# Batch 1's sums of q and k by pairs of tokens, raw weights by pairs of units, and fixed orders in the front of a fused attention and feed-forward kernel

## The chip, the core and the metric

The kernel runs on one core of a Trainium2 chip. Its time is the device time of one execution in microseconds (us). The core's engines are named as in the profile: PE (matrix products; PEld is its loading of weights), DVE (vector), ACT (activation functions), POOL (GpSimd) and SP (which here only starts transfers). Each works through its own queue in order, and they wait for one another by semaphores. All arithmetic is in float32; a product of full precision is made of three products of `fp32r` parts.

## What is computed

```
q_d, k_d, v_d = means of q, k, v over 4 neighbouring tokens       # q: (4 batches, 8 heads, 576 tokens, 64)
out_up    = repeat(softmax(q_d k_d^T / 8) v_d, 4)
out_local = softmax(q k^T / 8 where |i - j| < 4) v
x = (out_up + out_local) as (2304, 512)
x = (silu(x Wgate) * (x Wval)) Wout                               # inner width 1536
h = x Win;  out = (h * clip(h + 3, 0, 6) / 6) Wout2               # inner width 2048
```

The inputs are float64 in the reference; the five weight matrices reach the chip as 8-byte numbers, of which the kernel keeps the upper bits.

## The kernel before

**Blocks and units.** The 2304 tokens are cut into five blocks (512, 384, 512, 512 and 384 tokens). A block runs through 68 units, each a 128-wide piece of a weight matrix: G (gate), V (value), O (out), H, P, two of a kind after each other (G0 G1 V0 V1 G2 G3 V2 V3 O0 O1 ...). A unit of G, V or H over 512 columns is 12 products `pG`, `pV`, `pH` on PE.

**A unit's weights.** In block 0 a unit passes five steps that `prefetch(i)` gives out: `load_raw` (SP, into one of four `w64` buffers, in the page `w`), `decode_a` (ACT, `top`), `decode_b` (DVE, which joins the bits into `w32` and gives the `w64` buffer back), a write to HBM for the later blocks (`kept`, from ACT's queue), and, by pairs of units, `split_unit` (`wr`: the high part on ACT, the rest on DVE).

**The front.** `first_batch` makes batch 0's attention on PE before the units begin. `load_T` turns q and k; `down_scores`, `down_trans` and `down_values` (`fdS`, `fdT`, `fdO`) are the attention of the means, two heads at a time (c = 0 to 3). The local attention goes over five tiles of 122 tokens (the last has 88): `scores(i)` (`fS` on PE, its maximum `fnm` on DVE, eight exponentials into `held` on ACT), `norm(i)` (DVE), `trans(i)` (some filler products and the transposes `fPT` on PE, copied to `turned` by ACT and DVE), `values(i)` (`fO` on PE, then `xr` by ACT and DVE: the columns of the first block). The filler products compute nothing that is used; `FILL_P` says how many stand ahead of each `trans(i)`. PSUM has eight banks: `acc0` to `acc3`, two `mm`, `pa` and `px`. `down_trans` and `down_values` both use `pa` and `px`, `values` one of them; `fS` takes `acc0` and `acc1` or the two `mm`; `fPT` takes `acc2` and `acc3`, and each G or V unit one `mm`.

**Order.** A scheduler orders each engine's instructions when the program is built. Those that go through `tc.keep_in_program_order` (in `late`, `behind`, `together`) keep the order in which the code gives them; `behind` does so while `front[0]` is true.

**Batch 1's sums of 4** (`down_sums`) come from POOL's queue: the first of four tokens is loaded into `dn`, the other three are added to it by accumulating loads. Their transposes `pqT` and `pkT` follow on PE among the first units.

Of the kernel before, what the change touches and what calls it, by code (L numbers as in the profile page):

```python
# [32 lines left out]
HALVES = 1  # L33
# [10 lines left out]
FILL_P = (4, 8, 8, 8, 8)  # L44
# [3 lines left out]
def tile_kernel(  # L48
# [86 lines left out]

    def behind(ins):

        if front[0]:
            tc.keep_in_program_order(ins)
# [26 lines left out]
    def view(t, i):  # L166
        return t[:, i % 2, :].rearrange("p (c e) -> p c e", c=NC)

# [8 lines left out]
    def load_unit(i):  # L177
# [12 lines left out]
        if kind in "GVH":  # L190
            src = src[:, f * P * m:(f + 1) * P * m].rearrange("(c p) f -> p c f", p=P)
        else:
            src = src[f * P:(f + 1) * P, :].rearrange("p (c e) -> p c e", c=NC)
        if wide:
            raw[i] = sp.tile([P, 4 * DM + 32], I16, tag="w64", name=f"w64_{i}", bufs=4)
            behind(nc.sync.dma_start(raw[i][:, 1:1 + 4 * DM].rearrange("p (c e) -> p c e", c=NC), src))
        else:
            nc.sync.dma_start(view(w32[i // 2], i), src)
# [34 lines left out]
    def split_unit(i):  # L233
        if i % 2:
            return
        s = w32[i // 2].rearrange("p u (c e) -> p u c e", c=NC)
        r = sp.tile([P, 2, 2, NC, P], F32R, tag="wr", name=f"wr{i}", bufs=3)
        behind(nc.scalar.activation(r[:, :, 0], s, AF.Copy))  # L238
        behind(nc.vector.tensor_tensor(r[:, :, 1], s, r[:, :, 0].bitcast(F32), op=ALU.subtract))  # L239
        split[i], split[i + 1] = r[:, 0], r[:, 1]  # L240
# [29 lines left out]
    def put_cols(bi, col, xv):  # L270
# [4 lines left out]
        nc.scalar.activation(dst[:, :, 0], xv, AF.Copy)  # L275
        nc.vector.tensor_tensor(dst[:, :, 1], xv, dst[:, :, 0].bitcast(F32), op=ALU.subtract)
# [39 lines left out]


    def first_batch():
# [6 lines left out]
        with tc.tile_pool(name="fp", bufs=1) as fp:  # L325
# [125 lines left out]
            for base, sgn in ((-UPAD, -1), (UPAD + 3, 1)):  # L451
# [3 lines left out]
                )  # L455
            kT = fp.tile([P, NC, S + 6], F32, name="fkT")
            nc.vector.memset(kT[:, :, :3], 0.0)
            nc.vector.memset(kT[:, :, S + 3:], 0.0)
# [12 lines left out]
            def load_T(w, c):  # L471
                src = qn[w, c // 2]
                for th in range(2):
# [13 lines left out]
                    if w == "q":  # L487
                        nc.vector.tensor_scalar(dst, ps[:, :, :TT], 0.125, None, op0=ALU.mult)
                        nc.scalar.activation(small, ps[:, :, TT:], AF.Copy, scale=1 / 128)
                    else:  # L490
                        nc.scalar.activation(dst, ps[:, :, :TT], AF.Copy)
                        nc.vector.tensor_copy(small, ps[:, :, TT:])
# [7 lines left out]
            def down_scores(c):  # L500
# [14 lines left out]
                for par in range(2):  # L515
                    nc.vector.tensor_reduce(nm[:, par], pss[par], axis=AX.X, op=ALU.max, negate=True)
                    for half in range(2):
                        nc.scalar.activation(
# [6 lines left out]
            def down_trans(c):  # L525
                pd = dst[c]
                for par in range(2):
# [3 lines left out]
                    nc.scalar.activation(dpt[h], pt, AF.Copy)  # L531

            def down_values(c):
# [9 lines left out]
                nc.vector.tensor_scalar(sd, po[:, :, :, D:], EPS, 4.0, op0=ALU.add, op1=ALU.mult)  # L543
                nc.vector.reciprocal(sd, sd)
                nc.vector.tensor_tensor(
                    odN[:, :, 2 * c * D:2 * (c + 1) * D].rearrange("p g (a d) -> p g a d", a=2),
                    po[:, :, :, :D], sd.to_broadcast([NJH, 2, 2, D]), op=ALU.mult,
                )

# [4 lines left out]
            first_max = []  # L554

            def scores(i):
# [27 lines left out]
                for par in range(2):  # L584
                    ps = pss[par][:n, :, :w_]
                    nc.vector.tensor_reduce(nm[:n, :, par], ps, axis=AX.X, op=ALU.max, negate=True)
                    for c in range(NC):
                        nc.scalar.activation(
                            p_[:n, c, par, :w_], ps[:, c], AF.Exp, bias=nm[:n, c, par:par + 1],
                            accum_out=sm[:n, c, par:par + 1],  # L590
                        )
                pe[i], tot[i] = p_, sm
                if i == 0:
                    first_max.append(nm[:n, 0, :1])

            def norm(i):
                n = size(i)
                w_ = n + 6
                nc.vector.tensor_scalar(tot[i][:n], tot[i][:n], EPS, None, op0=ALU.add)
                nc.vector.reciprocal(tot[i][:n], tot[i][:n])  # L600
                nc.vector.tensor_tensor(
# [8 lines left out]
            def trans(i):  # L610
# [3 lines left out]
                for hh in range(2):  # L614
# [9 lines left out]
                    if hh:  # L624
                        nc.vector.tensor_copy(to, ps[:w_, :, :, :n])
                    else:
                        nc.scalar.activation(to, ps[:w_, :, :, :n], AF.Copy)
# [27 lines left out]
            for c in range(NC):  # L655
# [6 lines left out]
                if c == 2:  # L662
                    prefetch(3 - LR)
# [12 lines left out]
            down_trans(3)  # L676
            down_values(2)
            norm(1)
            scores(2)
            down_values(3)  # L680
            prefetch(5 - LR)
            values(0)
            for i in range(1, NT):
                next(ahead, None)
                next(ahead, None)
                trans(i)
                if i + 2 < NT:
# [5 lines left out]
                if i + 1 < NT:  # L693
                    norm(i + 1)
                next(ahead, None)
                values(i)
            for _ in ahead:
                pass
        front[0] = False
# [240 lines left out]
    HIGH, LOW = ((0, 0), (1, 0)), ((0, 1),)  # L940

    def run_unit(i):
# [3 lines left out]
        if kind in "GVH":  # L946
            ps = bank("mm", f"p{kind}{bi}_{f}", 2)[:, :nt]
            x = xr[bi] if kind != "H" else state["x2"]
            cols = [slice(0, nt)]
            if i < HALVES:  # L950
                cols = [slice(0, 244), slice(244, nt)]
            for cs in cols:
                for part in (HIGH, LOW):
# [203 lines left out]
```

## Time and profile before

| | |
|---|---|
| median of 3 runs | 967.41 us (967.27 to 970.9) |
| the profiled execution | 967.38 us |
| its span, first to last instruction | 965.7 us |
| PE busy, mean granted clock | 948.1 us, 0.993 |
| DVE, ACT, POOL busy | 724.6, 501.6, 110.4 us |

The time is the device's, the span runs from the first to the last instruction of the core; 1.7 us lie around it. A timeline row gives start, length (with the tail of the last instruction), engine, line, operation, result and inputs, shapes and count, and in brackets how long the engine had stood idle and what ended that. The granted clock is a share of 2.4 GHz.

### The profile page before, as it was taken

How to read it: one execution, taken by the hardware profiler on the slowest of the kernel's cores; microseconds unless marked ns; L12 is line 12 of the kernel's file. 1: busy time of each engine (PE TensorE's matmuls, PEld its weight loads, DVE VectorE, ACT ScalarE, POOL GpSimd, SP SyncE). 2: the span in 40 equal slices, each digit the busy share in tenths (PEclk: the TensorE clock that was granted, in tenths of full speed). 3: DMA queues.
4: the chain of work that ended last, by engine and by line, in shares of the span. 5: the costliest groups of instructions: out<-in, count | busy, mean ns of one | idle time of the engine just before them, and what ended most of it. 6: DMA issues, size and time to landing. Idle time of an engine off the chain costs nothing.

```text
span 965.7 us, 13166 instructions
## 1 busy us (share of the span) xinstructions
PE 948.1 (98%) x4928; PEld 803.2 (83%) x4928; DVE 724.6 (75%) x1059; ACT 501.6 (52%) x928; POOL 110.4 (11%) x125
## 2 busy tenths in 40 slices
PE   9899999999999999999999999999999999999997
PEld 7687888777899988878888778888888788999996
DVE  4678976899979979999774799997337994445652
ACT  4666566876543567553333764443335445444542
POOL 7610002200062300014320000000000000000000
PEclk9999999999999999999999999999999999999999
DMA  8999799866799823359972222462322323443331
GB/s 195 228 270 340 247 366 311 183 198 236 261 246 264 166 86 109 99 188 242 199 157 88 88 67 67 173 216 90 97 100 93 103 88 108 154 131 130 120 122 33
DMA packets 116340, 160.80 MB, mean 167 GB/s; under 512 B 61868, under 2 KB 83756, under 8 KB 116276
## 3 DMA queue, kind: packets, MB, share of 16 engines
q1 hardware_dynamic: 67892, 131.41, 42.7%
q0 software_dynamic: 43488, 10.72, 11.1%
q10 hardware_dynamic: 4896, 17.83, 4.7%
q8 instruction: 39, 0.64, 0.3%
q14 instruction: 25, 0.20, 0.1%
HBM read 137.29 MB, written 22.54 MB: 166 GB/s over the span
## 4 chain that ended last, share of the span: by engine, by line
PE 78%; DVE 7%; DMA 1%; ACT 1%; issue 1%; ACTq 0%; DVEq 0%
PE pH L956 19%; PE aP L998 18%; PE aO L998 13%; PE pV L956 13%; PE pG L956 12%; DVE wr L239 2%; PE pS L881 1%; PE pO L731 1%; DMA w<-in_moe_w_out_dram 1%; DVE xf L856 1%; PE pPT L724 1%; PE px L847 1%; DMA w<-in_moe_w_gate_dram 1%; DVE pv L827 1%; DVE w L225 1%
## 5 line engine op out<-in xcount | busy, mean ns | idle before, releaser
L239 DVE TENSOR_TENSOR wr<-w,wr 128x1024 fp32r<-128x1024 f32 x170 | 207.8, 1222 | 123.8 <-ACT wr L238 123.6
L238 ACT ACTIVATE wr<-w 128x1024 fp32r<-128x1024 f32 x170 | 179.5, 1056 | 119.1 <-issue 57.7
L956 PE MATMUL pH<-x,wr 128*128 128x512 f32 (+1 forms) x960 | 212.2, 372 | 0.0
L998 PE MATMUL aP<-wr,gH 128*128 128x512 f32 x864 | 211.4, 395 | 0.3 <-ACT gH L973 0.3
L956 PEld LDWEIGHTS pH<-x,wr 128*128 128x128 f32 x960 | 173.1, 188 | 25.3 <-issue 2.9
L998 PEld LDWEIGHTS aP<-wr,gH 128*128 128x128 f32 x864 | 159.8, 188 | 34.8 <-issue 2.5
L956 PE MATMUL pG<-xr,wr 128*128 128x512 f32 (+3 forms) x732 | 156.4, 369 | 1.0 <-DVE sl L968 0.6
L956 PE MATMUL pV<-xr,wr 128*128 128x512 f32 (+1 forms) x720 | 153.9, 369 | 0.9 <-ACT sl L962 0.9
L998 PE MATMUL aO<-gV,wr 128*128 128x512 f32 (+1 forms) x720 | 154.4, 371 | 0.0
L956 PEld LDWEIGHTS pG<-xr,wr 128*128 128x128 f32 x732 | 133.3, 191 | 18.5 <-DVE sl L968 1.0
L998 PEld LDWEIGHTS aO<-gV,wr 128*128 128x128 f32 x720 | 132.4, 190 | 16.9 <-DVE gV L974 0.2
L956 PEld LDWEIGHTS pV<-xr,wr 128*128 128x128 f32 x720 | 130.8, 188 | 18.4 <-ACT sl L962 1.8
L971 ACT ACTIVATE h<-pH,consts 128x512 f32<-128x512 f32 (+1 forms) x80 | 51.4, 643 | 59.7 <-PE pH L956 59.5
L973 ACT ACTIVATE gV<-sl 128x512 fp32r<-128x512 f32 (+1 forms) x60 | 35.0, 584 | 85.5 <-DVE sl L968 85.2
L216 ACT ACTIVATE top<-w 128x512 f16<-128x512 bf16 x68 | 52.3, 790 | 22.9 <-DMA w<-in_moe_w_out_dram 7.7
L962 ACT ACTIVATE sl<-pG 128x512 f32<-128x512 f32 (+1 forms) x60 | 33.0, 551 | 59.6 <-PE pG L956 57.0
L973 ACT ACTIVATE gH<-h 128x512 fp32r<-128x512 f32 (+1 forms) x80 | 46.9, 586 | 31.9 <-DVE h L972 31.6
L972 DVE SCALAR_TENSOR_TENSOR h<-h,pH 128x512 f32<-128x512 f32 (+1 forms) x80 | 50.5, 632 | 15.6 <-ACT h L971 15.1
L790 DVE TENSOR_TENSOR pr<-q,k 128x1792 f32<-128x1792 f32 x27 | 54.6, 2021 | 9.4 <-DMA k<-in_k_dram 9.2
L974 DVE TENSOR_TENSOR gH<-h,gH 128x512 fp32r<-128x512 f32 (+1 forms) x80 | 50.6, 633 | 10.9 <-ACT gH L973 10.5
L827 DVE TENSOR_TENSOR pv<-sc,v 128x1792 f32<-128x1792 f32 x27 | 54.6, 2022 | 0.5
L793 DVE TENSOR_REDUCE sc<-pr 128x28 f32<-128x1792 f32 x27 | 54.4, 2015 | 0.1
(131 smaller groups left out, 761.9 us busy)
## 6 DMA issues: line engine op xcount, KB each, us to landing
w<-kept SPq DMA_DIRECT2D x136, 512.0 KB
kept<-w ACTq DMA_DIRECT2D x34, 512.0 KB
w<-in_moe_w_out_dram SPq DMA_DIRECT2D x28, 512.0 KB
w<-in_moe_w_in_dram SPq DMA_DIRECT2D x16, 512.0 KB
w<-in_moe_w_gate_dram SPq DMA_DIRECT2D x12, 512.0 KB
w<-in_moe_w_val_dram SPq DMA_DIRECT2D x12, 512.0 KB
out_dram<-os SPq DMA_DIRECT2D x16, 256.0 KB
dnq<-in_q_dram POOLq DMA_DIRECT2D x24, 144.0 KB, 7.8
```

Source lines behind the costliest of these rows:

```text
L216: behind(nc.scalar.activation(halves(top[i % 2], 2, F16)[:, :, 1], h3.bitcast(BF16), AF.Copy))
L238: behind(nc.scalar.activation(r[:, :, 0], s, AF.Copy))
L239: behind(nc.vector.tensor_tensor(r[:, :, 1], s, r[:, :, 0].bitcast(F32), op=ALU.subtract))
L790: nc.vector.tensor_tensor(pr, qt[:, a:a + SUB, None, :].to_broadcast([P, SUB, W, D]), win(kt, a, SUB), op=ALU.mult)
L793: nc.vector.tensor_reduce(sc[:, a:a + SUB], pr, axis=AX.X, op=ALU.add)
L827: nc.vector.tensor_tensor(pr, pe[:, a:a + SUB, :, None].to_broadcast([P, SUB, W, D]), win(vt, a, SUB), op=ALU.mult)
L956: nc.tensor.matmul(ps[:, cs], r[:, a, c], x[:, c, b_, cs], start=part is HIGH and a == c == 0, stop=part is LOW and c == NC - 1,)
L971: nc.scalar.activation(h, ps, AF.Relu, scale=1 / 6, bias=half1[:, 0:1])
L972: nc.vector.scalar_tensor_tensor(h, h, 1.0, ps, op0=ALU.min, op1=ALU.mult)
L973: nc.scalar.activation(g[:, 0, :nt], h, AF.Copy)
L974: nc.vector.tensor_tensor(g[:, 1, :nt], h, g[:, 0, :nt].bitcast(F32), op=ALU.subtract)
L998: nc.tensor.matmul(ps, **one, start=f_ == 0 and a == b_ == 0, stop=f_ == nf - 1 and b_ == 1,)
```

## The change

Batch 1's sums of q and k (`pair_sums`) take two neighbouring tokens by one load: tokens 0 and 1 are loaded, tokens 2 and 3 are added by an accumulating load, and four additions on POOL join the two halves. A raw weight tile of G, V and H holds half the rows of two units where it held all rows of one; for all kinds a tile is now two runs for each partition. `split_unit` works on 1024 elements in a row. All of the front's work on DVE and ACT keeps the program's order, and so do the weight steps of the first four units of block 0. `scores` is cut in two, so that the exponentials (`weights`) have a place of their own. Two units begin inside the front (`begin_unit`), and there are 16 filler products where there were 36.

```diff
-HALVES = 1
+HALVES = 2
-FILL_P = (4, 8, 8, 8, 8)
+EARLY_W = 4
+FILL_P = (4, 4, 4, 4, 0)
...
+    class Ordered:
...
+            def issue(*args, **kw):
+                tc.keep_in_program_order(op(*args, **kw))
...
-            src = src[:, f * P * m:(f + 1) * P * m].rearrange("(c p) f -> p c f", p=P)
+            h = i % 2
+            src = src[h * DM // 2:(h + 1) * DM // 2, (f - h) * P * m:(f - h + 2) * P * m]
+            src = src.rearrange("(c p) f -> p c f", p=P)
...
+    def begin_unit(i, n):
+        kind, f, bi = units[i]
+        ps = bank("mm", f"p{kind}{bi}_{f}", 2)
+        products(ps, split[i], xr[bi], slice(0, n), tc.keep_in_program_order)
+        begun[i] = ps, n
...
+            vec, act = Ordered(nc.vector), Ordered(nc.scalar)
...
+            def pair_sums(b, gate):
...
+                            tok = tok.rearrange("h (j t) d -> j h t d", t=4)[:, :, t:t + 2]
+                            how = {"accum_op": ALU.add} if t else {}
+                            tc.keep_in_program_order(nc.gpsimd.dma_start(twos[w, half], tok, **how))
...
+                        nc.gpsimd.tensor_tensor(dn[w][:, half], st[:, :, 0], st[:, :, 1], op=ALU.add)
...
             scores(0)
-            ahead = down_sums(1, ["qk"], first_max[0])
+            ahead = pair_sums(1, first_max[0])
+            weights(0)
             down_trans(2)
             down_scores(3)
             scores(1)
+            weights(1)
             next(ahead)
             next(ahead)
+            norm(0)
             down_values(0)
             down_values(1)
-            norm(0)
+            scores(2)
             trans(0)
+            down_trans(3)
+            prefetch(3 - LR)
+            weights(2)
             prefetch(4 - LR)
-            down_trans(3)
-            down_values(2)
-            norm(1)
-            scores(2)
-            down_values(3)
-            prefetch(5 - LR)
-            values(0)
             for i in range(1, NT):
                 next(ahead, None)
                 next(ahead, None)
-                trans(i)
+                norm(i)
                 if i + 2 < NT:
                     scores(i + 2)
                 if i == 1:
-                    prefetch(6 - LR)
+                    down_values(2)
+                    down_values(3)
+                values(i - 1)
+                if i >= NT - HALVES:
+                    begin_unit(i - NT + HALVES, (i - 1) * QT)
+                trans(i)
+                if i + 2 < NT:
+                    weights(i + 2)
+                    prefetch(4 + i - LR)
...
+            values(NT - 1)
...
+            front[0] = i < EARLY_W
             prefetch(i)
```

The first place is ACT's queue between the first and the second tile's exponentials. `fdpT4` and `fdpT5` are the copies of `down_trans(2)` out of the banks `pa` and `px`, `fsm0` and `fsm1` mark the exponentials of tiles 0 and 1. Before:

```order
L531 ACTIVATE fdpT4_476<-fdT4_471 72x288
L588 ACTIVATE held_236,fsm0_445<-fS0_0_447,fnm0_446 122x128 x4
L588 ACTIVATE held_236,fsm0_445<-fS0_1_448,fnm0_446 122x128 x4
L531 ACTIVATE fdpT5_483<-fdT5_478 72x288
L518 ACTIVATE fdpd3_492<-fdS6_485,fdnm3_491 72x144 x2
```

Changed:

```order
L145 ACTIVATE held_236,fsm0_442<-fS0_0_444,fnm0_443 122x128 x4
L145 ACTIVATE held_236,fsm0_442<-fS0_1_445,fnm0_443 122x128 x4
L145 ACTIVATE fdpT4_473<-fdT4_468 72x288
L145 ACTIVATE fdpT5_480<-fdT5_475 72x288
L145 ACTIVATE fdpd3_489<-fdS6_482,fdnm3_488 72x144 x2
```

Both copies stand behind the eight exponentials of tile 0 now, where one stood ahead of them.

The second place is DVE's queue around the first pair's `wr` and `norm(2)` (the three rows with `fsm2`), which `trans(2)` waits for. Before:

```order
L225 SCALAR_TENSOR_TENSOR w32_0_580<-w64_1_257,top1_161 128x512
L599 TENSOR_SCALAR fsm2_612<-fsm2_612 122x8
L600 RECIPROCAL fsm2_612<-fsm2_612 122x8
L601 TENSOR_TENSOR held_236<-held_236,fsm2_612 122x1024
L239 TENSOR_TENSOR wr0_655<-w32_0_580,wr0_655 128x2x512
L276 TENSOR_TENSOR xr0_671<-fO0_658,xr0_671 128x4x122
L625 COPY turned_275<-fPT1_1_692 128x488
```

Changed:

```order
L291 TENSOR_TENSOR xr0_688<-fO0_675,xr0_688 128x4x122
L145 COPY turned_275<-fPT1_1_701 128x488
L237 SCALAR_TENSOR_TENSOR w32_0_622<-w64_1_257,top1_161 128x512
L252 TENSOR_TENSOR wr0_719<-w32_0_622,wr0_719 128x1024
L145 TENSOR_SCALAR fsm2_560<-fsm2_560 122x8
L145 RECIPROCAL fsm2_560<-fsm2_560 122x8
L145 TENSOR_TENSOR held_236<-held_236,fsm2_560 122x1024
```

`norm(2)` has moved behind `wr`, and both behind the work of `values(0)` and `trans(1)`. On ACT the matching part, which `wr` on DVE waits for, reads in the changed kernel:

```order
L145 ACTIVATE turned_275<-fPT1_0_691 128x488
L145 ACTIVATE held_236,fsm3_631<-fS3_0_633,fnm3_632 122x128 x4
L145 ACTIVATE held_236,fsm3_631<-fS3_1_634,fnm3_632 122x128 x4
L228 ACTIVATE top0_159<-w64_2_265 128x512
L251 ACTIVATE wr0_719<-w32_0_622 128x1024
```

Tile 3's exponentials stand between `trans(1)`'s copy and the `wr` of the first pair; before, `wr` stood ahead of that copy.

The third place is the end of the front on PE. Before:

```order
L644 MATMUL fO4_885<-turned_275,vw4_262 64x88 x2
L956 MATMUL pG0_0_921<-xr0_671,wr0_655 128x244 x8
L956 MATMUL pG0_0_921<-xr0_671,wr0_655 128x268 x12
L956 MATMUL pG0_1_957<-xr0_671,wr0_655 128x512 x12
L303 MATMUL pqT1_0_974<-ident_96,dnq1_526 128x72 x4
```

Changed (a run of 12 products `pG0_0` of 244 columns also stands ahead of `trans(3)`):

```order
L706 MATMUL fO3_851<-turned_275,vw2_259 64x122 x2
L340 MATMUL pG0_1_866<-xr0_688,wr0_719 128x366 x12
L682 MATMUL fPT4_0_879<-ident_96,held_236 94x88 x4
L682 MATMUL fPT4_1_885<-ident_96,held_236 94x88 x4
L700 MATMUL fO4_891<-tmp_186 128x88
```

Parts of the first two units have moved ahead of `trans(3)` and `trans(4)`, in the place of fillers; 12 products of 268 and 12 of 146 columns are left behind `fO4`.

## Rows read from the trace of the kernel before

**Rows 1.** Windows: length, busy us of each engine (instructions), granted clock, DMA.

```profile
25.20:71.10 45.90, 42.51 (x378) 34.47 (x377) 33.00 (x60) 29.73 (x104) 18.51 (x15) 0.93 1.15 242
71.10:90.20 19.10, 17.98 (x88) 14.15 (x87) 16.47 (x18) 12.46 (x20) 0.00 (x0) 1.00 0.96 350
...
33.70:37.10 3.40, 3.40 (x29) 2.93 (x27) 0.75 (x3) 0.00 (x0) 1.79 (x2) 0.50 1.35 264
64.40:67.90 3.50, 3.50 (x18) 3.50 (x18) 2.70 (x5) 2.61 (x5) 0.00 (x0) 0.51 0.98 382
```

**Rows 2.** Waits of PE from 71 us on: us in total, times, longest.

```profile
PE px L847 <- DVE o L833: 3.0, 4, 1.7
```

**Rows 3.** Timeline of PE, places where it stood or that others are measured against.

```profile
25.16 1.25 PE L538 MATMUL fdO<-fvd,fdpT 72*72 72x65 f32 x16
26.63 1.25 PE L538 MATMUL fdO<-fvd,fdpT 72*72 72x65 f32 x16 [0.22 <-ACT fdpT L531]
...
30.08 0.75 PE L724 MATMUL fdT<-ident,fdpd 72*72 72x72 f32 x8 [0.92 <-DVE tmp L545]
33.03 1.57 PE L538 MATMUL fdO<-fvd,fdpT 72*72 72x65 f32 x16 [2.21 <-ACT fdpT L531]
...
71.12 5.74 PE L956 MATMUL pV<-xr,wr 128*128 128x512 f32 x24
...
80.49 3.03 PE L956 MATMUL pG<-xr,wr 128*128 128x512 f32 x12 [0.57 <-DVE sl L968]
...
87.12 3.02 PE L956 MATMUL pV<-xr,wr 128*128 128x512 f32 x12 [0.54 <-ACT sl L962]
```

**Rows 4.** Timeline of PE, fillers to the end of values(1).

```profile
41.37 1.05 PE L469 MATMUL fPT<-ident 128*128 128x256 bf16 x8
42.26 1.00 PE L620 MATMUL fPT<-ident,held 122*128 122x122 f32 x8
43.19 0.64 PE L572 MATMUL fS<-band,pick 64*122 64x512 bf16 x4
...
44.63 0.48 PE L638 MATMUL fO<-tmp 72*128 72x122 f32 x2
...
47.73 1.05 PE L469 MATMUL fPT<-ident 128*128 128x256 bf16 x8
```

**Rows 5.** Timeline of ACT, one row for each kind of work.

```profile
23.41 0.37 ACT L588 ACTIVATE held<-fS,fnm 122x128 f32<-122x128 f32 x1
...
26.16 0.42 ACT L531 ACTIVATE fdpT<-fdT 72x288 f32<-72x288 f32 x1
...
31.85 0.82 ACT L216 ACTIVATE top<-w 128x512 f16<-128x512 bf16 x1
...
41.46 1.08 ACT L238 ACTIVATE wr<-w 128x1024 fp32r<-128x1024 f32 x1
...
68.08 1.28 ACT L962 ACT_TABLE_LOAD   x1 [1.06 <-DVE w L225]
```

**Rows 6.** Timeline of DVE, one row for each kind of work.

```profile
27.93 1.28 DVE L586 TENSOR_REDUCE fnm<-fS 122x4 f32<-122x512 f32 x2
...
39.28 0.68 DVE L225 SCALAR_TENSOR_TENSOR w<-w,top 128x512 int32<-128x512 int32 x1
...
41.38 0.20 DVE L600 RECIPROCAL fsm<-fsm 122x8 f32<-122x8 f32 x1
41.62 1.22 DVE L601 TENSOR_TENSOR held<-held,fsm 122x1024 f32<-122x1024 f32 x1
42.76 1.22 DVE L239 TENSOR_TENSOR wr<-w,wr 128x1024 fp32r<-128x1024 f32 x1
```

**Rows 7.** Timeline of POOL, an addition of the means of v.

```profile
21.10 1.27 POOL L412 TENSOR_TENSOR vd<-vd 72x512 f32<-72x512 f32 x1
```

**Rows 8.** DMA queue of POOL from 23 to 54 us: packets, MB, share of 16 engines.

```profile
q0 software_dynamic: 8552, 2.18, 69.8%
```

**Rows 9.** Timeline of SP, the load of the ninth unit's weights (w_8).

```profile
58.61 0.35 SPq L196 DMA_DIRECT2D w<-in_moe_w_out_dram x1
```

More of the change, by code (lines that the diff above doesn't have):

```diff
@@ L315, in down_T, with products @@
             yield
+    HIGH, LOW = ((0, 0), (1, 0)), ((0, 1),)
+    begun = {}
+    def products(ps, r, x, cs, pin=lambda ins: None):
+        for part in (HIGH, LOW):
+            for c in range(NC):
+                for a, b_ in part:
+                    pin(nc.tensor.matmul(
+                        ps[:, cs], r[:, a, c], x[:, c, b_, cs],
+                        start=part is HIGH and a == c == 0, stop=part is LOW and c == NC - 1,
+                    ))
+    def begin_unit(i, n):
[3 more added lines that the diff above has]
+        begun[i] = ps, n
     def first_batch():
@@ L548, in down_values @@
                 )
+            def pair_sums(b, gate):
+                tc.keep_in_program_order(nc.gpsimd.tensor_copy(consts[:gate.shape[0], 60:61], gate))
+                twos = {}
+                for t in range(0, 4, 2):
+                    for w, src in (("q", q), ("k", k)):
+                        for half in range(2):
+                            if not t:
+                                st = fp.tile([TT, GT, H // 2, D], F32, tag="fnat", name=f"two{w}{half}", bufs=4)
+                                st = st.rearrange("p a h d -> p (a h d)")[:NJH, :2 * H * D]
+                                twos[w, half] = st.rearrange("p (h t d) -> p h t d", h=H, t=2)
+                            tok = src[b, :, half * NJH * 4:(half + 1) * NJH * 4, :]
+                            tok = tok.rearrange("h (j t) d -> j h t d", t=4)[:, :, t:t + 2]
+                            how = {"accum_op": ALU.add} if t else {}
+                            tc.keep_in_program_order(nc.gpsimd.dma_start(twos[w, half], tok, **how))
+                        yield
+                for w in "qk":
+                    dn[w] = sp.tile([NJH, 2, H, D], F32, tag="dn" + w, name=f"dn{w}{b}", bufs=1)
+                    for half in range(2):
+                        st = twos[w, half]
+                        nc.gpsimd.tensor_tensor(dn[w][:, half], st[:, :, 0], st[:, :, 1], op=ALU.add)
+                    yield
             def size(i):
@@ L554, in first_batch @@
             first_max = []
+            scored = {}
             def scores(i):
@@ L584, in scores, with weights @@
                 for par in range(2):
[L585 to L591, printed above, removed]
+                    vec.tensor_reduce(nm[:n, :, par], pss[par][:n, :, :w_], axis=AX.X, op=ALU.max, negate=True)
                 pe[i], tot[i] = p_, sm
+                scored[i] = pss, nm
                 if i == 0:
                     first_max.append(nm[:n, 0, :1])
+            def weights(i):
+                n = size(i)
+                pss, nm = scored.pop(i)
+                for par in range(2):
+                    for c in range(NC):
+                        act.activation(
+                            pe[i][:n, c, par, :n + 6], pss[par][:n, c, :n + 6], AF.Exp,
+                            bias=nm[:n, c, par:par + 1], accum_out=tot[i][:n, c, par:par + 1],
+                        )
             def norm(i):
@@ L937, in tile_kernel @@
     state = {}
-    HIGH, LOW = ((0, 0), (1, 0)), ((0, 1),)
     def run_unit(i):
@@ L946, in run_unit @@
         if kind in "GVH":
-            ps = bank("mm", f"p{kind}{bi}_{f}", 2)[:, :nt]
+            ps, done = begun.pop(i, (None, 0))
+            if ps is None:
+                ps = bank("mm", f"p{kind}{bi}_{f}", 2)
             x = xr[bi] if kind != "H" else state["x2"]
[L949 to L953, printed above, removed]
-                    for c in range(NC):
-                        for a, b_ in part:
-                            nc.tensor.matmul(
-                                ps[:, cs], r[:, a, c], x[:, c, b_, cs],
-                                start=part is HIGH and a == c == 0, stop=part is LOW and c == NC - 1,
-                            )
+            products(ps, r, x, slice(done, nt))
+            ps = ps[:, :nt]
             if kind == "G":
```

66 lines of the change are left out of this document (33 added, 33 removed).

## The prediction

> **What bounds the kernel.** PE does. The windows view splits the run at the first V unit: in the 45.9 us from 25.2 to 71.1, the last part of the front with G0 and G1, PE is busy for 42.5 us [rows 1]. After that the list of PE's waits has little: the most is 3.0 us for DVE ahead of `px`, in four pieces [rows 2]. The timeline has a wait of 0.57 us ahead of G3 and one of 0.54 us ahead of V3 [rows 3]. So behind the first few units the change can only shift a stream of products that already stands back to back, and what is to be won or lost lies in some 65 us.
>
> There the reader is to see two kinds of loss. PE stands for 45.9 - 42.5 = 3.4 us, the largest piece 2.21 us ahead of a `fdO` that waits for ACT's `fdpT` [rows 3]. And the granted clock is 0.50 in two stretches of about 3.4 us, one just behind that wait, one at the end of the front without any wait, where PE did only the last tile's small products [rows 1]. 0.50 is the 1.2 GHz level; the same products at 2.4 GHz would have taken half as long, so the two cost 3.4 us together (the mean of 0.93 over 45.9 us says 3.2). Work at full clock in this stretch is 45.9 - 3.4 - 3.3 = 39.2 us.
>
> **Fillers and early units.** 20 fillers go. Eight take from 41.37 to 42.26, 0.11 us each [rows 4]: -2.2 us. G1 is cut in two like G0, 12 more products for the same columns. Nothing shows a product of 146 columns; at no overhead it costs nothing, at most what a whole product takes (5.74 us for 24 give 0.24 [rows 3]), 12 x 0.24 = 2.9 us. A matmul's time here is near its columns, so I take 0.2. PE's work becomes 37.2 us.
>
> **New waits, by the fixed orders.** I walk the queues with the old durations. A row's length holds some 0.1 to 0.15 us of tail that the next instruction overlaps (ACT's `wr` lasts 1.08, the next one starts 0.93 later); in a chain I count from start to start.
>
> First: both `fdpT` copies of `down_trans(2)` stand behind tile 0's exponentials. `fdO` of c = 0 writes the bank `pa`, so it now waits for the first copy. The exponentials begin at 23.41 and the next instruction at 26.16, 2.75 us for eight; the copy takes 0.42 [rows 5]: 26.6. PE is free at 25.16, when it began `fdO` before [rows 3], so it stands 1.4 us.
>
> Second: `values(0)` writes `pa` again and waits until DVE has read `fdO` of c = 2. From the end of `trans(0)` PE has `fdT` (0.6), `fS` (43.19 to 44.63, 1.4 [rows 4]) and two `fdO` (1.1 each): 4.3 us. The other chain is `fdT`, two copies (0.7), `top` (0.65), DVE's joining step (0.6), `norm(1)` (0.2 + 0.2 + 1.2), the maximum of tile 3 (1.2) and the `fdO` steps (0.7): 6.0 us [rows 5, 6]. PE stands 1.7 us.
>
> Third: `trans(2)` waits for `norm(2)`, which stands behind `wr`. From the end of `trans(1)` on: eight exponentials 2.75, `top` 0.65, `wr` 0.95 on ACT, then `wr` 1.15 and `norm(2)` 1.6 on DVE, 7.1 us [rows 5, 6]. PE meanwhile has `fS` of the small tile (1.1), `values(1)` (44.63 to 47.73, 3.1) and four fillers 0.45 [rows 4]: 4.65. It stands 2.5 us.
>
> Fourth, at the end of the front: from the end of `fO4` ACT does two `xr` (0.4), `top`, `wr`, the table load (1.28) and the first `sl` (0.55), 3.85 us, and only then is V0's bank free. PE waits 0.3 us for the first `xr`, and has 1.5 us of G0, 0.85 of G1 and 0.2 of transposes: 2.85. It stands 1.0 us more. Before, ACT loaded that table from 68.08 on, and V0 began at 71.12 without a wait [rows 3, 5].
>
> Sum: 37.2 + 1.4 + 1.7 + 2.5 + 1.3 = 44.1 us against 45.9: -1.8. The waits ahead of G3 and V3 (0.57 + 0.54) came from DVE and ACT being busy with early weight steps and batch 1's first products; in the new order their inputs come 0.6 to 1.4 us before PE gets there: -1.1. Together -2.9.
>
> **The clock.** All stretches above are at 2.4 GHz. The last tile's small products now have dense G products on both sides, so I let the fall at 64.4 go. But PE stands three times for 1.4 to 2.5 us among small products, and the one row of such a case is the fall right behind the wait of 2.21 us [rows 1, 3]. Nothing at all costs a wait if the clock holds; 1.7 us each (3.4 us at half) if it falls behind it. I take one fall, at the third and longest wait, as nearest to that row: +1.7. Forecast: 967.4 (the profiled execution's 967.38, whose median of runs is 967.41) - 2.9 + 1.7 = 966.2 us.
>
> The Trainium skill, in "TensorE: Matmul & The Clock Gate", section "HAM oscillation — how this bites in real kernels", has gaps between short bursts lower the clock again and again. By it all three waits would count, three times 1.7: 969.6 us. The trace is milder, as the wait of 0.92 us ahead of 30.08 was followed by no fall of its own before the longer one came [rows 3].
>
> **Batch 1's sums.** Eight loads go, and each of the eight left brings twice the bytes in pieces twice as long. POOL's queue took 69.8% of the DMA engines from 23 to 54 us [rows 8], so the DMAs have more room. No PE wait of this stretch is for a DMA, and the sums are needed only by `pqT` behind G1; the price is 0, and it was 0 before. Four additions of 1.27 us [rows 7] follow on POOL, 5.1 us. The loads were over by about 54, `pqT` comes near 69, so some 10 us are to spare; without that cover `pqT`, and V0 behind it, would wait for POOL.
>
> **Raw weights.** Transfers with half the pieces and `wr` on 1024 elements in a row: `wr` has the same element count, and I price it at 0 (its 1.22 us are the same as those of `norm`'s 1024 contiguous elements [rows 6]). But with fixed orders the step for w_4 on DVE comes only behind `values(4)`, near 67.5. SP holds the load of w_8 until then, and batch 1's q, k, v loads queue behind it: it was at 58.61 [rows 9], and will be 9 us later. DVE's first products of batch 1 start some 6 us later in turn. Walked on: from 73.2 DVE has the first `sl`, a product of 2.0, one `gV` step, two joining steps and the second `sl`, so `wr` for V2 ends at 79.5, and PE gets there at 81.5; in the same way `wr` for O0 ends 0.9 and that for V4 1.1 us before its unit. So it is hidden, by about 1 us.
>
> **Rivals.**
> - *The clock holds* at every wait: 964.5 us; if two waits come out at half length too, 962. For it: the clock was still full after the wait of 0.92 us [rows 3]. Against: the fall at 33.7 [rows 1]. Chance 0.22.
> - *POOL's additions and DVE hold each other up.* Four times 1.27 us fall around 40 to 47 us, where DVE's joining step, `wr` and `norm(2)` are the third wait's chain. Nothing shows a cost: POOL's additions of v ran when DVE had only copies and maxima. Bounds 0 and 5.1 us, 966.2 to 971.3. Chance 0.11. The Trainium skill, "SBUF — State Buffer", section "Who interferes with whom", says that a DVE instruction with two SBUF inputs contends with a GpSimd instruction that reads SBUF, and `norm` and `wr` are such. No run here shows it yet.
> - *Weights come too late.* If a load of w_8 to w_12 or DVE's first products slip by 2 to 5 us, the margin of 1 us is gone and the O or V units wait 1 to 4 us: 967 to 970, more if it repeats. Chance 0.05.
> - *Slower than before: the clock stays down.* With fewer fillers and PE standing three times, the half rate could hold for much of 26 to 66 us. Each us at 1.2 GHz costs half of one. It decides from (967.4 x 0.005 + 2.9) x 2 = 15.5 us at half rate on, 972.2 us; at 20 us it would be 974.5. Against: before, both falls were over after 3.4 us although only small products followed the first. Chance 0.07.
>
> **How the numbers follow.** One fall: 0.55, by itself 964.5 to 968.5 (a wait off by 1.5 us, or a second fall). 0.5% of the time, 4.8 us, is what a measurement can tell from no change: under 962.6 or over 972.2. Below lies a third of the first rival, 0.08. Above lie the last rival and 0.02 of the others, 0.09. Same: 0.83. The range from 963.0 to 970.5 leaves out about 0.1 on each side: the best of a holding clock, the worst of POOL and the clock.
>
> **What would show it.** In the new profile PE's waits should name `fdO` for `fdpT` (1.4 us near 26), `fO` for the `fdO` step on DVE (1.7 near 37), `fPT` for `held` (2.5 near 48) and `pV` for `sl` (1.0 near 69), none above 0.3 us from there to 100 us. A stretch at clock 0.50 should stand behind the third wait, none near 65. V0 should begin near 71, and POOL's additions be over before 50. It is wrong if PE waits for `wr` or `top` after 70 us, if `norm` or `wr` on DVE last over 1.3 us, or if the half rate covers more than two stretches.

## The result, and the profile after

The changed kernel takes 974.6 us (median of 20 runs, 968.08 to 983.29), the kernel before 967.34 in the runs beside them (20, 963.83 to 971.01): a ratio of 1.0077, interval 1.0052 to 1.0102. It is slower, and above the predicted range. Its profiled execution took 972.05 us with a span of 970.2, so it lies below the median. The ratio and the means below leave out the two longest of these 20 runs and the longest of `cover`, which lie more than 1.5% above the fastest run of their kernel; the expectations still count them.

The waits of PE in the changed kernel from 24 us on (us in total, times, longest), and the places of the front in PE's timeline:

```profile
PE px L911 <- DVE o L897: 4.6, 5, 1.9
PE fO L700 <- DVE fdsd L145: 1.9, 1, 1.9
PE fdO L572 <- ACT fdpT L145: 1.5, 1, 1.5
PE fPT L682 <- DVE held L145: 1.4, 1, 1.4
PE pV L340 <- ACT sl L1017: 0.9, 1, 0.9
PE pG L340 <- ACT xr L290: 0.8, 2, 0.5
PE pG L340 <- DVE sl L1023: 0.8, 1, 0.8
PE pO L795 <- DMA dnv<-in_v_dram: 0.7, 1, 0.7
```

```profile
27.03 2.26 PE L572 MATMUL fdO<-fvd,fdpT 72*72 72x65 f32 x32 [1.51 <-ACT fdpT L145]
38.17 0.76 PE L700 MATMUL fO<-tmp 72*128 72x122 f32 x2 [1.88 <-DVE fdsd L145]
53.14 1.05 PE L682 MATMUL fPT<-ident,held 122*128 122x122 f32 x8 [1.38 <-DVE held L145]
74.16 5.74 PE L340 MATMUL pV<-xr,wr 128*128 128x512 f32 x24 [0.94 <-ACT sl L1017]
```

All four waits of the walk are there, and they name what it named. V0 begins at 74.16, 3 us later than before [rows 3]. The windows say why (length, busy us of each engine, granted clock, DMA):

```profile
25.20:74.10 48.90, 42.80 (x374) 33.82 (x372) 27.33 (x54) 27.81 (x103) 13.39 (x12) 0.90 0.71 155
37.80:48.00 10.20, 9.83 (x56) 6.98 (x56) 2.81 (x7) 3.27 (x15) 6.11 (x5) 0.50 1.15 157
259.60:263.00 3.40, 3.40 (x10) 2.65 (x9) 2.65 (x7) 1.23 (x3) 0.00 (x0) 0.50 0.42 139
...
64.40:67.90 3.50, 3.42 (x29) 3.02 (x29) 1.19 (x2) 0.69 (x2) 0.00 (x0) 1.00 0.00 0
```

From the wait of 1.88 us on the clock is at 1.2 GHz for 10.2 us, which is 5.1 us by the clock; the fall at 64 us [rows 1] is gone. The span is 4.5 us longer and V0 begins 3.0 us later, so a third of the loss lies where the prediction didn't look, behind two waits far from the front. In PE's timeline:

```profile
191.47 0.71 PE L795 MATMUL pO<-pT,dnv 72*64 72x144 f32 x6 [0.68 <-DMA dnv<-in_v_dram]
...
259.25 0.41 PE L911 MATMUL px<-ident,o 128*128 128x128 f32 x2 [1.90 <-DVE o L897]
```

`pO` (the first product with batch 1's sums of v) waits for their loads. `px` waits for `o`, a fall of 3.4 us follows, and DVE's timeline shows what made `o` late: a joining step and a `wr` stand ahead of it, and the joining step itself waited 2.00 us until the write to `kept` gave its buffer back. In the kernel before, a joining step that didn't wait stands there, and no `wr` (the last two rows); `px` waits at most 0.4 us there.

```profile
256.94 0.69 DVE L237 SCALAR_TENSOR_TENSOR w<-w,top 128x512 int32<-128x512 int32 x1 [2.00 <-DMA kept<-w]
257.55 1.22 DVE L252 TENSOR_TENSOR wr<-w,wr 128x1024 fp32r<-128x1024 f32 x1
258.69 0.42 DVE L897 TENSOR_TENSOR o<-pv 128x256 f32<-128x256 f32 x1
...
250.91 0.69 DVE L225 SCALAR_TENSOR_TENSOR w<-w,top 128x512 int32<-128x512 int32 x1
251.52 0.42 DVE L833 TENSOR_TENSOR o<-pv 128x256 f32<-128x256 f32 x1
```

The kernel before has a like loss further on. One of its `px` waits 1.70 us, and 3.4 us at half rate follow; the same wait in the changed kernel has no fall behind it. So between these two traces the falls behind `px` cancel. First the row of the kernel before and its window, then those of the changed kernel:

```profile
343.66 0.41 PE L847 MATMUL px<-ident,o 128*128 128x128 f32 x2 [1.70 <-DVE o L833]
344.10:347.50 3.40, 3.40 (x13) 3.40 (x12) 3.06 (x8) 0.79 (x2) 0.00 (x0) 0.53 0.45 154
...
350.08 0.41 PE L911 MATMUL px<-ident,o 128*128 128x128 f32 x2 [1.70 <-DVE o L897]
350.10:353.60 3.50, 3.50 (x21) 3.50 (x22) 3.43 (x9) 1.39 (x3) 0.00 (x0) 1.00 0.41 149
```

### The profile page after: what moved, and what is told of

It reads as the page before. It is cut to its first block, busy times and chain, and to the rows that moved or that the text cites. A ratio compares the mean times of both kernels' runs of the same rounds, so it can differ in the third digit from the quotient of the medians.

```text
span 970.2 us, 13165 instructions
## 1 busy us (share of the span) xinstructions
PE 948.5 (98%) x4920; PEld 802.2 (83%) x4920; DVE 723.7 (75%) x1059; ACT 502.2 (52%) x928; POOL 106.0 (11%) x121
## 3 DMA queue, kind: packets, MB, share of 16 engines
q1 hardware_dynamic: 57652, 131.41, 40.8%
q0 software_dynamic: 37408, 10.71, 10.2%
## 4 chain that ended last, share of the span: by engine, by line
PE 80%; DVE 10%; DMA 4%; ACT 2%; issue 2%; POOL 0%; SPq 0%; ACTq 0%; DVEq 0%; POOLq 0%
PE aP L1053 15%; PE pH L340 14%; PE pG L340 14%; PE pV L340 14%; PE aO L1053 14%; DMA dnv<-in_v_dram 3%; DVE wr L252 2%; DVE pv L891 2%; DVE xf L920 1%; DVE h L1027 1%; DVE pv L895 1%; PE fO L700 1%; PE pO L795 1%; PE pS L945 1%; DMA k<-in_k_dram 1%
## 5 line engine op out<-in xcount | busy, mean ns | idle before, releaser
L340 PE MATMUL pG<-xr,wr 128*128 128x512 f32 (+5 forms) x744 | 155.3, 363 | 1.7 <-ACT xr L290 0.8
```

The costliest lines, as they stand in the source:

```text
L340: pin(nc.tensor.matmul(ps[:, cs], r[:, a, c], x[:, c, b_, cs], start=part is HIGH and a == c == 0, stop=part is LOW and c == NC - 1,))
```

## The experiments

Every run gives its time and its mean granted clock. I split each time into *clock*, time x (1 - granted clock), and *rest*, what is left. In the traces 0.9 to 2.4 us of the first lie at the very end, where PE has no more work, in every kernel. Means over runs ± their standard error; the ratio is to the runs of before beside them.

| kernel | runs | mean | clock | rest | ratio, interval |
|---|---|---|---|---|---|
| before | 129 | 969.1 | 8.0 ± 0.3 | 961.1 ± 0.2 | |
| changed | 18 | 975.0 | 11.6 ± 0.8 | 963.4 ± 0.6 | 1.0077 [1.0052, 1.0102] |
| fill36 | 6 | 979.6 | 13.7 ± 1.6 | 965.9 ± 0.5 | 1.0100 [1.0052, 1.0149] |
| cover | 11 | 976.5 | 7.1 ± 1.1 | 969.4 ± 0.8 | 1.0076 [1.0042, 1.0110] |
| sumv25 | 12 | 974.4 | 11.2 ± 0.7 | 963.2 ± 0.4 | 1.0051 [1.0022, 1.0080] |
| cover_sumv | 12 | 969.6 | 4.2 ± 0.9 | 965.4 ± 0.6 | 1.0010 [0.9985, 1.0035] |
| wait2 | 8 | 975.0 | 11.2 ± 0.5 | 963.8 ± 0.5 | 1.0063 [1.0033, 1.0092] |
| oldsums | 12 | 968.9 | 4.6 ± 0.5 | 964.3 ± 0.5 | 0.9997 [0.9976, 1.0017] |
| norm_early | 12 | 968.5 | 6.3 ± 0.7 | 962.2 ± 0.4 | 0.9988 [0.9961, 1.0015] |
| pieces1k | 6 | 979.7 | 15.5 ± 1.2 | 964.2 ± 0.5 | 1.0110 [1.0066, 1.0154] |
| apart | 6 | 980.4 | 14.7 ± 1.3 | 965.7 ± 1.1 | 1.0127 [1.0083, 1.0170] |
| free | 12 | 974.8 | 13.2 ± 0.4 | 961.5 ± 0.6 | 1.0060 [1.0038, 1.0082] |
| early0 | 6 | 976.1 | 13.8 ± 0.6 | 962.3 ± 0.7 | 1.0072 [1.0044, 1.0100] |
| bsums | 12 | 968.8 | 8.3 ± 1.0 | 960.5 ± 0.5 | 0.9996 [0.9966, 1.0025] |
| bpairs | 12 | 969.6 | 8.7 ± 1.1 | 961.0 ± 0.9 | 1.0008 [0.9979, 1.0038] |
| bfill16 | 12 | 966.7 | 7.8 ± 1.0 | 958.9 ± 0.5 | 0.9960 [0.9925, 0.9994] |
| bbest | 12 | 969.1 | 10.2 ± 1.0 | 959.0 ± 0.4 | 1.0000 [0.9976, 1.0024] |
| bcover | 12 | 966.7 | 4.3 ± 0.5 | 962.5 ± 0.6 | 0.9981 [0.9954, 1.0007] |
| bcover16 | 12 | 963.9 | 3.8 ± 0.6 | 960.1 ± 0.3 | 0.9956 [0.9931, 0.9980] |

So the changed kernel loses 3.6 us by the clock and 2.3 in the rest, 5.9 in all. The prediction had -1.6 and +0.4. (The 20 runs of before beside the changed kernel have no clock on record and aren't among the 129; their mean is 967.6, and against them the loss is 7.4.)

**The changed kernel again (after_again), and more or fewer fillers.** Theory A is the clock behind the waits; B, the waits and orders alone; C, the order of DVE behind the front.

> The changed kernel once more, nothing edited, to see where the half rate lies in another execution. Theory A (the waits of PE in the front bring the clock down, for longer than the 3.4 us that I took): a stretch at 0.50 of 6 us or more somewhere from 26 to 60 us, right behind one of the three waits for fdpT, fdsd or held, and V0 near 74 us. Rival B (the waits themselves and the order behind the front cost the time, the clock does not): the half rate in the front lasts 3.4 us or less, V0 begins near 71 to 72 us, and the loss comes behind it. Rival C (an unlucky order of DVE's work behind block 0's O units): px waits 1.9 us for o near 259 us again.

It took 972.79 us. The half rate ran from 28 to 31.4 us, behind the first wait, and for 10 us from 38 us on; `px` waited 2.1 us. A and C both hold.

```diff
-FILL_P = (4, 4, 4, 4, 0)
+FILL_P = (4, 8, 8, 8, 8)
```

> The changed kernel with the 36 filler products of the kernel before at their old places; every other instruction keeps its place. 20 products of 0.11 us are 2.2 us of PE's work, 0.9 us of it ahead of trans(1) and trans(2), the other 1.8 us less ahead of trans(3) and trans(4); those ahead of trans(2) stand in the wait for held and cost nothing. Theory A with the fillers as the cause: the clock holds behind the waits, 0.992 or more in the mean, 967 to 970 us, 4 to 7 us less than the 974.6 of the changed kernel. Theory A with the waits as the cause: the fillers stand behind the waits for fdpT and fdsd, so the fall comes as before, 974 to 977 us. Rival B: 974.6 plus 1.8 us, 976.4.

No faster, with a fall of 6.8 us from 39 us on, behind the wait of `values(0)` as before: more fillers elsewhere don't help, and none of them stands in that wait.

> The kernel before with the 16 filler products of the changed kernel and nothing else (the scheduler then orders some of DVE's and ACT's work in the front anew). 20 products of 0.11 us go, 2.2 us. Theory A with the fillers as the cause: the half rate grows from 6.8 us in the front to 10 us or more, and the time rises by 1 to 6 us, 968 to 973. If the fillers had no part in the clock: 964.5 to 966 us, a little faster than before. Rival B expects the second too.

16 fillers in the kernel before save 2.2 us of rest and, in the mean of 12 runs, cost nothing by the clock (7.8 us against 8.0). The one trace, of a long run (971.64), has 17.1 us at half rate in the front and by itself would have said the opposite. The missing fillers are not the cause.

**Fillers inside the waits (cover).**

```diff
+            fill(bank("acc0", "cover0"), 12)
             down_values(0)
...
+                if i == 1:
+                    fill(bank("acc2", "cover1"), 16)
                 values(i - 1)
...
+FILL_P = (4, 0, 22, 4, 0)
```

> The changed kernel with fillers inside the three waits: 12 ahead of down_values(0) (they write acc0, which the first tile's exponentials free before the copies), 16 ahead of values(0) (in the bank that trans(1) takes next), 22 ahead of trans(2) in place of 4; the other orders are unchanged. In the waits they cost nothing: 1.3, 1.7 and 2.3 us of products. Theory A: PE has no idle piece above 0.6 us from 26 to 60 us, the clock stays at 1.00 there, V0 begins near 69 to 70 us, and the median comes to 966 to 969 us, 6 to 8 us less than the changed kernel. Rival B: the waits are only filled and not shortened, so the time stays at 973 to 976 us whatever the clock does. Rival C: px waits 1.9 us near 254 as before, and about 3 us of the loss remain: 969 to 971.

The clock's share fell from 11.6 to 7.1 us, as A says, but the rest rose by 6, and the time stayed, some 8 us above A's range. The waits of its PE show where:

```profile
PE pO L798 <- DMA dnv<-in_v_dram: 5.3, 1, 5.3
PE px L914 <- DVE o L900: 4.4, 4, 1.9
PE fPT L682 <- DVE held L145: 2.6, 1, 2.6
```

This led to theory D: `pO` waits for `dnv`.

**Earlier sums of v (sumv25), and both (cover_sumv).**

```diff
-SUMV = 31
+SUMV = 25
```

> The changed kernel with SUMV = 25 in place of 31: the eight loads that make batch 1's sums of v (dnv) start behind the product of V9 and not of V11, some 30 us earlier; the order on every engine is unchanged. Theory A (the waits of the front and the clock behind them) expects no change: 974 to 976 us. Theory D (the larger pieces of the raw weight loads hold up POOL's queue, so dnv lands late and the first pO waits for it, 0.7 us in the changed kernel, 2.1 and 5.3 us in two relatives of it, and longer in the slow half of the executions, with a clock fall behind it): no wait of pO for dnv, and a median of 969 to 971 us with a narrower spread, none above 977. Rival C (px waits for o near 259 us, behind a DVE that waits for the write of kept): that wait stays, so theory D alone can't come below 968.

The wait of `pO` went, and no run of 12 is over 977.24, where 8 of the changed kernel's 20 are; but the median stays at 975.03. That fits D for the long runs, not for the bulk.

> The fillers inside the three waits and SUMV = 25 together. A run's time is split in two: what the clock costs (time x (1 - mean granted clock)) and the rest. Means so far: before 8.1 + 961.4 us, changed 12.3 + 963.5, the changed kernel with fillers in the waits 7.5 + 969.6, with SUMV = 25 alone 11.2 + 963.2. Theory A for the clock (PE standing three times in the front lowers it, and fillers there keep it up) and theory D for the rest (the gain of the fillers is lost again where pO waits for dnv, 5.3 us): 7.5 for the clock and 964.5 to 965.5 for the rest, 972 to 973 us. If the two have nothing to do with each other's place and the rest of the fillers' 6 us is their own work: 7.5 + 969, 976.5 us.

Level with the kernel before, and 3 us better than D and A had it: without the wait of `pO`, the fall behind it (6.8 us at half rate in `cover`) goes too. The window of the front (24 to 76 us) is at full clock throughout:

```profile
24.00:76.00 52.00, 47.65 (x441) 38.66 (x438) 31.61 (x58) 31.15 (x109) 13.99 (x12) 1.00 0.76 181
```

V0 begins 1.9 us earlier than in `sumv25`, which has 10.2 us at half rate in its front. First the row of `sumv25`, then that of `cover_sumv`:

```profile
73.68 5.74 PE L340 MATMUL pV<-xr,wr 128*128 128x512 f32 x24 [0.94 <-ACT sl L1017]
71.79 5.74 PE L340 MATMUL pV<-xr,wr 128*128 128x512 f32 x24 [0.95 <-ACT sl L1020]
```

**Size of pieces (pieces1k), and the loads by pairs undone (apart).** D blamed the larger weight pieces.

```diff
-            src = src.rearrange("(c p) f -> p c f", p=P)
+            src = src.rearrange("(c p) (g f) -> p c g f", p=P, g=2)
```

> The changed kernel with the same raw weight loads cut into pieces of 1 KB (four for each partition) where it has 2 KB; the data and their places are the same. Theory D by the size of the pieces: dnv lands 1 to 2 us earlier, as in the kernel before (5.8 us for a load in place of 6.2 to 6.6), pO waits less than 0.3 us, 969 to 972 us. If the size of the pieces has no part in it: pO waits as before, 973 to 976 us. Theory A expects 973 to 976 us too.

The trace has the same 57,652 packets in SP's queue as the changed kernel (`apart`, where the pieces lie apart, has 67,892). So this is the changed kernel once more by its transfers. It shows how far the mean of six runs can lie, 979.7 us against 975.0, and so how little the other kernels with six runs say by their times alone. And it shows how long the wait can be, with a fall of some 10 us behind it:

```profile
PE pO L795 <- DMA dnv<-in_v_dram: 6.5, 1, 6.5
```

> The changed kernel with the raw weights loaded and split as in the kernel before (a tile for each unit, four runs of 1 KB for each partition for O and P); the order on every engine is that of the changed kernel. So far pO waited for dnv in all eight traces of kernels with weights by pairs but for those whose sums of v start earlier (0.5 to 6.5 us), and in none of four without. Theory D by the loads: no wait of pO, 11 to 12 us for the clock and 961.5 to 962.5 for the rest, none over 978 us, 973 to 974. If the front's new order makes dnv late: pO waits 0.5 us or more in the trace and the time stays at 12.3 + 963.5 us, 975 to 976.

`pO` still waits, 2.5 us, and the time is no better. The loads by pairs aren't needed for a late `dnv`; D keeps the wait and loses its cause. From 158 to 190 us, beside the sums of v, 9.56 MB moved here, 8.10 in the changed kernel and 7.36 in the kernel before; that this traffic is the cause wasn't tried.

**One part of the change alone.**

> The kernel before with the raw weights by pairs of units alone (two runs of 2 KB for each partition, wr on 1024 elements in a row); every engine keeps its order. Theory D: dnv lands later than before, pO waits 0.5 to 5 us for it, and the time rises by 2 to 6 us against the kernel before (about 969): 971 to 975. Theory A: no change, 967 to 969.5 us. My prediction's price for this part was 0, with the margin of some weights down to 1 us.

> The kernel before with batch 1's sums of q and k by pairs of tokens alone (eight loads and four additions on POOL in place of sixteen loads); every other engine keeps its order. My prediction's price was 0; its rival of POOL against DVE gave up to 5 us more. Theory A and theory D expect no change: 967 to 969.5 us against about 969 for the kernel before. POOL against DVE: DVE's norm, wr and joining steps in 40 to 50 us last over 1.3 us in place of 1.22, and 970 to 974 us.

Neither moves the time beyond its interval of some 0.3%, as the prediction's prices of 0 had it. But the trace of `bpairs` shows a wait of 2.7 us for `dnv`, and none of the six traces of the old order without the pairs has one, so the pairs may have a part in it. And `bsums` says nothing of POOL against DVE: in its trace the product of `norm` and `wr` take 1.22 and 1.23 us, but the additions fall from 45.5 to 53.8 us, where DVE has neither of the two.

**Orders left free (free, early0).**

```diff
-            vec, act = Ordered(nc.vector), Ordered(nc.scalar)
+            vec, act = nc.vector, nc.scalar
...
-EARLY_W = 4
+EARLY_W = 0
```

`free` has both edits and unpinned columns' parts, `early0` the second alone.

> The changed kernel with the orders of DVE and ACT in the front left to the scheduler: no fixed order for the front's vector and activation work, the columns' parts and the weight steps of the first four units; PE's order in the front, the pair sums, the weights by pairs and the 16 fillers stay. Theory A (the fixed orders make the three waits, these lower the clock): no wait for fdsd or held above 0.5 us, 8 to 9 us for the clock and 960 to 962 for the rest, 968 to 971 us. If the loss is of the units that begin inside the front or of the loads: as the changed kernel, 12 + 963.5.

My form of theory A falls: without fixed orders PE stands even longer (7.9 us from 24 to 76), for `turned`, `tmp` and `fdpT`, and the clock costs 13.2 us. That fits the standing as the cause, whoever orders it.

> The changed kernel with EARLY_W = 0: the weight steps of block 0's first units are free again, all of the front stays fixed. The three waits of the front stay, so theory A expects the clock's 12 us to stay. Theory C (the orders behind the front, which put DVE's joining step and its wait for the write of kept ahead of o, cost 1.9 us of px's wait): a new order of DVE without that wait gives 961.5 to 962 for the rest, 973 to 974 us; with it 963.5 and 975 to 976.

In both, `px` waits 0.4 to 0.6 us near 250 us, so C has its place. The rest falls by 1.1 ± 0.9 and 1.9 ± 0.8, which agrees with its size but is hardly clear of the noise.

**The second wait alone (wait2), the additions (oldsums) and norm(2) (norm_early).**

> The changed kernel with SUMV = 25 and 16 fillers in the second wait alone (ahead of values(0), those of trans(1) moved there, so 12 more in all). If the second wait is the one that brings the clock down: 5 to 6 us for the clock and 963.5 to 964.5 for the rest, 969 to 970 us. If any of the three waits is enough: 9 to 11 for the clock, 973 to 975, and the half rate starts behind the wait for fdpT near 28 us or that for held near 52 us.

The wait moved: the second is gone, `fPT` now waits 5.4 us, and 14 us at half rate begin there; the first, 1.5 us, has no fall behind it. The clock costs 11.2 us, as it did with the second wait in place. With the clock held ahead of it, the third wait is 5.4 us behind the changed kernel's four fillers, not 2.5. PE's row and DVE's timeline here, and POOL's beside it:

```profile
52.24 1.89 PE L682 MATMUL fPT<-ident,held 122*128 122x122 f32 x8 [5.37 <-DVE held L145]
...
46.73 1.90 DVE L252 TENSOR_TENSOR wr<-w,wr 128x1024 fp32r<-128x1024 f32 x1 [3.08 <-ACT wr L251]
48.56 1.22 DVE L145 TENSOR_SCALAR fsm<-fsm 122x8 f32<-122x8 f32 x1
49.81 0.20 DVE L145 RECIPROCAL fsm<-fsm 122x8 f32<-122x8 f32 x1
50.05 2.13 DVE L145 TENSOR_TENSOR held<-held,fsm 122x1024 f32<-122x1024 f32 x1
```

```profile
45.06 2.49 POOL L603 TENSOR_TENSOR dnq<-twoq 72x512 f32<-72x512 f32 x2 [3.27 <-DMA twoq<-in_q_dram]
47.65 3.45 POOL L603 TENSOR_TENSOR dnk<-twok 72x512 f32<-72x512 f32 x2
```

> The changed kernel with fillers in its three waits and SUMV = 25 (4.2 us for the clock and 965.4 for the rest, 969.6 in the mean), with batch 1's sums of q and k again by sixteen loads and no addition on POOL; no other engine's order changes. If POOL's additions hold DVE up: the step on fsm is back at 0.16 us and the product into held at 1.22, the third wait falls from 2.7 to 0.7 us, and the rest to 963.2 to 963.8: 967 to 968 us. If they don't: 2.7 us stay and 969.6.

Without the additions the same four DVE steps take:

```profile
46.59 1.23 DVE L252 TENSOR_TENSOR wr<-w,wr 128x1024 fp32r<-128x1024 f32 x1 [3.08 <-ACT wr L251]
47.73 0.23 DVE L145 TENSOR_SCALAR fsm<-fsm 122x8 f32<-122x8 f32 x1
48.00 0.20 DVE L145 RECIPROCAL fsm<-fsm 122x8 f32<-122x8 f32 x1
48.24 1.23 DVE L145 TENSOR_TENSOR held<-held,fsm 122x1024 f32<-122x1024 f32 x1
```

The third wait fell from 2.7 to 0.8 us: the additions and DVE do hold each other up, 2.6 us in `wait2`. The rest fell by 1.1 ± 0.8 and the mean by 0.7 us, so how much of it reached the end is not shown.

> The changed kernel with fillers in the first two waits, SUMV = 25, and norm(i + 1) given out ahead of weights(i + 2) and the weight steps, so that norm(2) no longer stands behind wr; with no wait to cover, trans(2) has 4 fillers again in place of 22. If the place of norm(2) makes the third wait: none above 0.3 us for held, 2.7 us of standing and 2.0 us of fillers go, 960.5 to 961.5 for the rest and 4 to 5 for the clock: 965 to 966 us, 3 us faster than the kernel before. If DVE or ACT only come late elsewhere (G0 waiting for wr, or V0 for sl): 968 to 970.

The wait for `held` is gone and the rest falls by 3.2, but new ones come (`fO` for `turned` 1.4 us, a `pG` for `sc` 2.5 near 316 us) and the trace has four short falls (one behind `px`, as in `cover_sumv`): 968.5 us, level with the kernel before.

**The remedy in the kernel before (bbest, bcover, bcover16).**

> The kernel before with 16 fillers and batch 1's sums by pairs of tokens, and nothing else: 16 fillers alone gave 7.8 + 958.9 us (966.7 in the mean), the sums alone 8.3 + 960.5 against 8.1 + 961.4 for the kernel before. If both hold side by side: 8 + 958.5, 966 to 967 us, 2 to 3 us faster than the kernel before and 8 us faster than the changed one. If the fillers are needed where the sums' additions fall: 968 to 970.

The rest is near what was expected, the clock is worse (10.2 ± 1.0 us), and nothing is won.

```diff
+            fill(bank("acc0", "cover0"), 8)
             down_trans(3)
+            fill(bank("acc0", "cover1"), 18)
             down_values(2)
```

> The kernel before with 26 more fillers in its own two waits of the front: 8 ahead of down_trans(3) (it stood 0.92 us there) and 18 ahead of the fdO that stood 2.21 us; they write acc0, which is free by then, and every other instruction keeps its place. Theory A: no half rate from 32 to 48 us (3.4 us in one trace of the kernel before, 14 to 18 in three near relatives of it), 4 to 5.5 us for the clock in place of 7.5 to 8.1, and the rest at 961 to 961.5: 965.5 to 967 us, 2 to 3 us faster than the kernel before. If the waits don't bring the clock down there: 969 us.

```profile
24.00:76.00 52.00, 49.95 (x451) 39.82 (x447) 38.68 (x67) 35.34 (x117) 20.31 (x18) 1.00 1.17 275
```

No half rate in the front (0.93 there in the trace of before), none before 958 us. The mean is 2.4 us lower, 966.7, but the interval of the ratio, 0.9954 to 1.0007, still holds 1.

> The same 26 fillers in the kernel before with the 16 fillers elsewhere and batch 1's sums by pairs of tokens (that kernel without them took 10.2 us for the clock and 959.0 for the rest, 969.1 in the mean). Theory A: 5 to 6 us for the clock, 959 to 960 for the rest, 964 to 966 us, the fastest of all. If the other fillers hold the clock: as without them, 969.

This one, old orders with pair sums, 16 fillers and 26 in PE's two waits, beats both kernels: 963.2 us in the median, a ratio of 0.9956 to the kernel before, interval 0.9931 to 0.9980.

## Why the prediction was wrong

**The step that failed** is "I take one fall, at the third and longest wait: +1.7". The front had 10.2 us at half rate, which is 5.1, and they began at the second wait. Over all runs the clock's share rose by 3.6 us where the prediction had it fall by 1.6, so this term is off by 5.2 of the 7.1 us between the forecast change of -1.2 and the 5.9 of the table. The rival "the clock stays down" (0.07) was the case in kind. Three pairs of kernels that differ by fillers in the waits show that the clock hangs on these waits: its share goes from 11.2 to 4.2 (`sumv25`, `cover_sumv`), 8.0 to 4.3 (before, `bcover`) and 10.2 to 3.8 (`bbest`, `bcover16`). I had read one trace of before, in which the fall at 33.7 was 3.4 us long [rows 1]; in `bsums` and `bbest`, with the same wait, the half rate lasts 13.6 and 17.0 us. The estimate that the prediction made by the Trainium skill ("TensorE: Matmul & The Clock Gate", "HAM oscillation — how this bites in real kernels"), 969.6 us with a fall of 1.7 at each of three waits, lies nearer by its number and not by what happened: the trace has one long fall. That section's case is also another one, with waits longer than the bursts of products between them; here a wait of 1.88 us behind 9.3 us of products was enough, and the measurement decides.

**The third wait, and luck.** From 25.2 us to V0 the sum was 44.1 us without the clock, and the trace gives 48.9 - 5.1 = 43.8. That they agree is luck. The third wait was forecast at 2.5 us and came out at 1.4 because PE, at half rate ahead of it, came late. With the clock held it is 5.4 us behind the same four fillers (`wait2`). POOL's additions, priced at 0, make most of the difference: without them 0.8 us are left behind 22 fillers (`oldsums`), some 2.9 behind four (18 fillers are 2.1 us). So the rival of POOL and DVE was real, and hidden in the changed kernel, where the additions end at 49.8 us and `wr` begins at 50.28; for `wr` and the product into `held` the traces agree with the Trainium skill, "SBUF — State Buffer", "Who interferes with whom". The fall and this wait hide each other: without the fall V0 comes 1.9 us earlier (`sumv25`, `cover_sumv`), not 5.1.

**The second step** that failed is "behind the first few units the change can only shift a stream of products". The scheduler orders DVE anew behind the front, and `px` near 259 us waits 1.9 us for `o`, with a fall of 3.4 us at half rate (1.7) behind. And `pO` waits for `dnv`, 0.7 us here and up to 6.5 in another trace. Why `dnv` is late stays open: it is late without the weights by pairs (`apart`) and with them alone (`bpairs`).

**What held.** The four waits and what they wait for; pair sums and weights by pairs at 0 (`bsums`, `bpairs`). Of the 1.1 us for G3 and V3 only V3's came: G3 still waits 0.8 for `sl`. The end of the front had no fall, but not for the reason given. The prediction read the old fall at 64.4 as one of the last tile's small products; the 18 products of that row [rows 1] are those of G0 and G1, which run from 64.11 on. And `bsums`, `bfill16`, `bbest` and `bcover`, with the old end of the front, have no fall there either.

**Open.** Which of the three waits starts the fall: it began behind the first, the second or the third in different traces. `free` and `early0` have more half rate from 64 to 85 us; there PE stands again for `turned` (1.6 and 2.4 us in `free`, 2.0 in `early0`), but the last fall of `early0` has no such wait ahead of it. Nor has the old fall at 64.4 us, so a fall can also come without a wait.

## What to carry to other kernels

A wait of 1.4 to 2.2 us among small products is priced at itself plus the chance of a fall of the clock, and the fall at several traces' worth, not one: here it was 3.4 us in one trace and 17 in a near relative, and some such waits had none. The arithmetic share of a fall is not what its removal gives back, since a faster PE comes earlier to its next wait. Put products that write a free bank into the wait itself: 26 to 42 more of them took 3.7 to 7 us off the clock's share and added 1 to 2 us of rest, 2.4 to 5.2 us less in the mean. When orders change early in a program, compare the order of the busiest helper engine far behind too, and look for chains of loads that end without margin.

## What the runs showed of the hardware

- While POOL added two SBUF tiles, DVE's steps on SBUF took longer: one on 122x8 1.22 us in place of 0.23, one on 1024 elements 2.13 in place of 1.23 (`wait2`, `oldsums`), and POOL's two additions 3.45 in place of 2.49 (`wait2`).
- Cutting the transfers into adjacent pieces of 1 KB left the packets of the queue as they were (57,652 in `pieces1k` and the changed kernel).
- The same wait of 1.70 us ahead of `px` was followed by 3.4 us at half rate in the trace of the kernel before and by none in that of the changed kernel.
